# Loading and gating a linear recurrence by chunks of 1024 tokens instead of windows of 512

## The chip, the core and the metric

The kernel runs on one core of a Trainium2 chip. Its engines work side by side, each through a queue of its own, in order: TensorE (PE: matrix multiplies and transposes into PSUM; PEld is its loading of weights), VectorE (DVE), ScalarE (ACT), GpSimd (POOL) and SyncE (SP), which here only issues transfers. Sixteen DMA engines carry the transfers. They are tied together by semaphores. The metric is the device time of one execution in microseconds; the time of the kernel before is 302.48 us, the median of three runs (301.65 to 303.43).

## What is computed

The input has 4 sequences of 6336 tokens with 256 features, 25344 tokens in all. A gated linear recurrence runs along each sequence, and a gated unit with a causal convolution follows:

```python
sig_r, sig_i = 1/(1+exp(-r_gate)), 1/(1+exp(-i_gate))
a_t = exp(8 * sig_r * log(clip(a_base, 1e-6, 1-1e-6)))    # a_base = sigmoid(a_param), per feature
x_gated = sqrt(max(1 - a_t*a_t, 1e-6)) * sig_i * x
h = a_t[:, t] * h + x_gated[:, t];  y[:, t] = h            # for every token t, h starts at 0
gate = sigmoid(sum over k of conv_w[k] * y shifted)        # 5 taps, causal
out = (gate * (y @ w_val)) @ w_out
```

All inputs and the output are float32; the kernel works in bfloat16 between the stages.

## The kernel before

Tokens are cut into windows of at most 512 (`wins`, numbered 0 to 50) and windows into chunks (`CHUNKS`, L16): chunks 0 and 1 are one window of 256, chunk 2 one of 512, chunks 3 to 25 two windows of 512 each (windows 3 to 48), chunks 26 and 27 one window of 512 and one of 256. Work on the two gates' inputs and on the gated unit goes by windows, the recurrence by chunks. Sigmoids are computed as 0.5 + 0.5 tanh(x/2), so that tangent and exponential share one table of ScalarE; the square root needs another table, and `BATCHES` (L19) says which chunks share one visit to it.

The order of the work is written out by hand in `ORDER` (L33): one word for each step, with its window or chunk, the half of the features where there are two (.0 or .1), and behind an @ its PSUM banks. The loop at L504 emits the words one after the other, and every engine takes its own instructions in that order. It loads another table where the next word needs it (L509). The words:

- lr, li, lx (L276 to L283, `load` at L267): SP issues the load of a window of r, i or x, 512 KB each for 512 tokens, in pieces of 4 KB for each of 128 partitions (token 4p+j of the window lies in partition p). They go to two rings of four windows, `riring` and `xring`.
- th (L286): ACT takes the tangent of both gates of one window in one operation, 2048 columns of `riring` to `tring`. `tring` (L203) has three places of three halves for each window: `swapped` (L263) makes two successive windows of one place use them in turn, so that the tangents of r stay longer than those of i.
- pp (L295), up (L307): POOL adds 1 to the tangent of i and multiplies with x into `uring`, the ring of gated inputs, ten windows (`NU`). For some windows PE copies x to PSUM (xp, L311) and DVE does both in one operation (uv, L319).
- tr (L326), ex (L339): PE transposes the tangents of r to features by tokens, ACT takes the exponential into `aring`. `GROUPS` says which two chunks share one operation.
- sq on POOL, sa on ACT (L356, L364): the square of a. rt (L368): ACT takes the root for one batch.
- nt (L383), xg (L396), xt (L401): PE transposes the roots back to tokens by features, DVE multiplies them into `uring`, PE transposes the product.
- sc (L415): DVE runs the recurrence of a chunk as a scan, 1024 columns for each half.
- cv (L435), tg (L448), vl (L452), gv (L461), ou (L466): the convolution on PE, its tangent on ACT, y @ w_val on PE, the gate's product on DVE, the last product on PE, each for a window. cd or ca (L484, L487) copies the result out of PSUM, on DVE or on ACT, and st (L490) stores it, issued by SP.

A load waits until its place in the ring has been read: lr and li of a window for the tangent four windows back, lx for the product with x four windows back. A store waits for its copy, and loads behind it in SP's queue wait with it.

```python
    dst = riring[:, w % NRI, "ri".index(which) ^ swapped(w), 0:J, :]
nc.sync.dma_start(dst, flat[which][wstart[w]:wstart[w] + n, :].rearrange("(p j) d -> p j d", p=P))
...
nc.scalar.activation(out=tring[:, w % NTRI, a:a + 2, 0:J, :], in_=riring[:, w % NRI, :, 0:J, :],
                     func=ACT.Tanh, scale=0.5)
...
if table.get(name, have) != have:
    have = table[name]
    nc.scalar.preload_act_table_set(have)
```

Of the kernel before, what the change touches and what calls it, by code (L numbers as in the profile page):

```python
# [8 lines left out]
P = 128  # L9
# [14 lines left out]
NU = 10  # L24
NRI = 4
NX = 4
NTRI = 3
# [6 lines left out]
s_ident s_small s_kt s_diag li.2 lr.2 th.2 lr.3 lr.0 li.0 th.0 pp.0 tr.2.0@0 li.1 lr.1 tr.0.0@1 ex.2.0 th.1 lx.0 lx.2  # L34
li.3 up.0 tr.2.1@2 ex.2.1 tr.0.1@0 ex.0.0 tr.1.1@3 ex.1.1 tr.1.0@4 sq.1.1 ex.0.1 sq.0.1 lx.3 xp.3@0,1 lx.1 lr.6 th.3
sq.0.0 rt.0 lr.5 sq.2.0 pp.2 up.2 nt.0@5 xg.0 xt.0@2,3 li.5 th.5 sq.2.1 li.6 lr.4 uv.3 th.6 pp.6 pp.5 xp.1@5 sc.0.0
sc.0.1 cv.0@2,3 uv.1 li.4 th.4 tg.0 s_wl.1 ex.1.0 lx.4 li.7 tr.3.1@0,1 s_wl.0 lr.7 ex.3.1 lx.5 tr.3.0@2,3 ex.3.0
s_wl.3 lx.6 lx.7 pp.4 up.4 th.7 lr.9 rt.2 xp.7@2,3 li.8 uv.7 sa.4.0 sq.4.1 sq.3.1 sq.1.0 rt.1 nt.2@0 xg.2 nt.1@1 xg.1
s_wl.2 lr.8 li.10 lx.8 xt.2@2,3 xt.1@0,1 sc.1.1 li.9 lr.10 sq.3.0 rt.3 li.11 up.6 sc.1.0 lx.10 lr.11 sc.2.1 sc.2.0
up.5 th.8 lx.11 s_wcast th.10 lx.9 pp.10 up.10 lr.14 th.9 li.13 li.14 lr.13 xp.8@4,5 li.12 lr.12 uv.8 th.11 li.15  # L40
nt.3@0,1 xg.3 nt.4@6,7 pp.11 up.11 cv.1@2,3 tg.1 xg.4 xt.3@0,1 sc.3.1 vl.1@4,5 tr.5.0@6,7 ex.5.0 sq.5.0 tr.5.1@2,3
gv.1 ou.1.0@1 cd.1.0 st.1 lx.12 lr.15 ex.5.1 vl.0@4,5 xp.9@6,7 th.14 sq.5.1 cv.2@2,3 sc.3.0 th.13 uv.9 lx.13 xt.4@1,0
gv.0 ou.0.0@4 cd.0.0 st.0 sc.4.1 lx.15 cv.3@6,7 th.12 li.16 li.18 tr.7.1@4,5 tg.2 vl.2@2,3 gv.2 tg.3 ex.7.1 sq.6.1
sq.6.0 lx.14 pp.14 pp.12 up.12 tr.7.0@6,7 ex.7.0 sq.7.0 lx.16 cv.4@2,3 tg.4 th.15 ou.2.0@4,5 cd.2.0 sc.4.0 st.2 lr.18
lr.16 vl.3@6,7 xp.13@2,3 vl.4@4,5 gv.4 sq.7.1 rt.4 uv.13 th.16 sq.8.1 sq.8.0 pp.15 up.15 li.17 lr.17 up.14 ou.4.0@4,5
li.19 cv.5@0,1 lr.19 gv.3 cd.4.0 lx.17 tg.5 ou.3.0@6,7 lx.18 st.4 cd.3.0 st.3 nt.5@4,5 li.20 xg.5 pp.16 up.16 th.17
pp.17 lr.20 nt.7@6,7 xg.7 lx.19 li.21 nt.6@2,3 xg.6 th.18 pp.18 lr.21 xt.5@4,5 sc.5.1 up.17 vl.5@6,7 cv.6@0,1 tg.6
th.19 tr.9.1@2,3 ex.9.1 li.22 lr.22 up.18 sq.9.1 pp.19 gv.5 sc.5.0 tr.9.0@6,7 ex.9.0 lx.20 ou.5.0@0,1 cd.5.0 sq.10.1
xt.6@5,4 up.19 sc.6.1 cv.7@0,1 tg.7 cv.8@2,3 th.20 lr.24 tg.8 sc.6.0 vl.6@6,7 gv.6 xt.7@0,1 cv.9@4,5 ou.6.0@6,7 sc.7.0
th.21 tg.9 cd.6.0 vl.7@2,3 gv.7 vl.9@6,7 th.22 tr.11.0@0 sc.7.1 ou.7.0@2,3 vl.8@4,5 sq.9.0 tr.12.0@1 gv.9 ou.9.0@6,7  # L50
gv.8 ou.8.0@4,5 sq.10.0 st.5 cd.7.0 cd.9.0 lx.22 st.6 rt.5 lx.21 nt.8@6,7 lr.23 li.23 cd.8.0 nt.9@4,5 pp.22 pp.21
up.22 pp.20 up.20 up.21 xg.8 ex.12.0 xg.9 ex.11.0 li.24 st.7 st.9 li.25 lr.25 lx.23 lx.24 li.26 lr.26 th.23 xt.8@6,7
sc.8.0 sq.11.0 pp.23 sq.12.0 lr.27 li.27 cv.11@2,3 tg.11 cv.10@4,5 sc.8.1 cv.12@0,1 st.8 th.24 pp.24 tg.10 tg.12
vl.11@2,3 tr.11.1@6 ex.11.1 gv.11 vl.10@4,5 gv.10 th.25 xt.9@0,1 sc.9.0 tr.12.1@2 ex.12.1 ou.11.0@6,7 cd.11.0
ou.10.0@4,5 cd.10.0 cv.14@2,3 up.23 lx.25 lx.27 th.26 nt.10@6,7 sc.9.1 st.11 li.29 st.10 tg.14 tr.13.0@4,5 xg.10 up.24
sq.11.1 th.27 ex.13.0 tr.13.1@2,3 vl.12@0,1 gv.12 sq.12.1 li.30 lr.30 lx.26 pp.25 pp.27 sq.13.0 xt.10@6,7 sc.10.1
ex.13.1 sq.13.1 up.27 sq.14.0 pp.26 up.25 lr.28 cv.13@4,5 tg.13 vl.13@0,1 gv.13 li.28 vl.14@2,3 gv.14 ou.12.0@4,5
cd.12.0 ou.13.0@0,1 cd.13.0 ou.14.0@2,3 cv.15@4,5 lr.29 st.13 lx.28 lr.31 sc.10.0 cv.16@0,1 cd.14.0 rt.6 nt.11@6,7
tg.15 tg.16 xg.11 vl.15@2,3 gv.15 th.28 st.12 li.31 lx.29 sq.14.1 up.26 nt.13@4,5 xg.13 pp.28 up.28 nt.12@0,1 xg.12
li.32 vl.16@2,3 gv.16 lx.31 lr.32 lx.30 xt.11@4,5 sc.11.1 sc.11.0 ou.15.0@6,7 th.30 pp.30 th.29 pp.29 cv.18@0,1  # L60
ca.15.0 lr.34 li.34 up.29 cv.17@2,3 tg.18 xt.12@6,7 tg.17 vl.17@0,1 gv.17 tr.15.1@2,3 tr.15.0@4,5 th.31 sc.12.0
ou.17.0@0,1 cd.17.0 sc.12.1 ex.15.1 ex.15.0 cv.20@2,3 tg.20 li.33 lr.33 ou.16.0@0,1 cd.16.0 th.32 vl.18@4,5 gv.18
pp.31 up.31 th.34 xt.13@2,3 sc.13.1 vl.19@6,7 cv.19@0,1 tg.19 gv.19 st.17 st.14 st.16 st.15 up.30 th.33 sq.16.1 lx.32
sc.13.0 li.35 lr.35 lx.33 ou.18.0@4,5 cd.18.0 lx.34 li.36 sq.15.0 lr.38 cv.21@0,1 sq.15.1 vl.21@6,7 st.18 lx.35 lr.36
tg.21 gv.21 vl.20@0,1 sq.16.0 cv.22@2,3 gv.20 li.38 lr.37 li.37 pp.34 ou.19.0@4,5 cd.19.0 pp.33 pp.32 up.32
ou.21.0@6,7 ou.20.0@0,1 rt.7 cd.21.0 st.21 tg.22 cd.20.0 nt.14@4,5 xg.14 st.19 nt.16@6,7 xg.16 vl.22@0,1 gv.22 th.35
up.33 up.34 pp.35 tr.17.1@2,3 ex.17.1 xt.14@4,5 sc.14.0 sc.14.1 tr.17.0@6,7 ex.17.0 cv.23@0,1 cv.24@2,3 tg.23 tg.24
ou.22.0@6,7 cd.22.0 nt.15@0,1 xg.15 vl.24@2,3 vl.23@4,5 gv.23 st.20 st.22 lx.36 gv.24 up.35 cv.26@6,7 sq.17.1 th.36
pp.36 sq.18.0 th.38 xt.15@0,1 sc.15.0 sc.15.1 th.37 pp.37 sq.18.1 sq.17.0 ou.23.0@4,5 tg.26 ca.23.0 cv.25@2,3 tg.25
tr.19.0@6,7 ex.19.0 sq.19.0 xt.16@4,5 sc.16.0 tr.19.1@2,3 ex.19.1 sc.16.1 cv.27@0,1 ou.24.0@6,7 cd.24.0 tg.27  # L70
vl.25@2,3 vl.26@0,1 sq.19.1 rt.8 cv.28@4,5 gv.26 up.36 sq.20.1 li.39 st.23 lx.38 lr.40 pp.38 gv.25 lx.37 vl.27@6,7
gv.27 ou.26.0@0,1 cd.26.0 ou.25.0@2,3 lr.41 lr.39 tg.28 th.39 st.24 cd.25.0 ou.27.0@6,7 cd.27.0 nt.19@0,1 nt.17@2,3
xg.17 xg.19 cv.29@6,7 tg.29 sq.20.0 up.37 up.38 nt.18@4,5 xg.18 vl.28@2,3 gv.28 vl.29@6,7 gv.29 xt.17@0,1 sc.17.1
li.40 th.40 tr.21.1@4 li.41 th.41 pp.40 pp.39 st.26 st.25 tr.21.0@5 ex.21.1 ex.21.0 lx.39 li.42 ou.29.0@6,7 ca.29.0
lr.42 sc.17.0 st.27 lx.40 xt.18@2,3 up.39 th.42 ou.28.0@4,5 cv.30@6,7 cd.28.0 tg.30 tr.22.1@0 ex.22.1 tr.22.0@1
sq.21.0 sq.21.1 up.40 cv.32@6,7 ex.22.0 sq.22.1 tg.32 sc.18.1 cv.31@4,5 tg.31 lr.43 st.29 sc.18.0 li.43 th.43
vl.30@0,1 vl.31@6,7 gv.30 vl.32@4,5 gv.32 gv.31 ou.30.0@0,1 cd.30.0 xt.19@3,2 sc.19.0 ou.31.0@6,7 sq.22.0 rt.9
ou.32.0@4,5 st.28 cd.32.0 cd.31.0 lr.44 sc.19.1 lx.41 lx.43 lr.45 pp.42 pp.43 pp.41 up.41 li.44 up.43 lr.46 li.46
lx.42 up.42 st.30 cv.33@0,1 li.45 vl.33@4,5 tg.33 st.32 gv.33 nt.21@6,7 th.44 nt.20@0,1 xg.20 lx.45 lr.47 li.48 lr.48
th.46 pp.44 xg.21 nt.22@2,3 xg.22 lx.44 cv.35@4,5 th.45 pp.45 pp.46 up.45 st.31 li.47 ou.33.0@0,1 ca.33.0 tg.35  # L80
xt.20@6,7 sc.20.0 tr.23.1@2,3 ex.23.1 sc.20.1 cv.34@0,1 tg.34 cv.36@4,5 sq.24.1 tg.36 vl.35@2,3 gv.35 vl.36@0,1 gv.36
tr.23.0@6,7 vl.34@2,3 gv.34 ou.35.0@4,5 cd.35.0 lx.46 st.33 up.44 xt.21@0,1 sq.23.1 th.48 pp.48 ex.23.0 sq.24.0
sc.21.0 sc.21.1 th.47 cv.38@2,3 tg.38 ou.36.0@4,5 ou.34.0@6,7 ca.36.0 sq.23.0 ca.34.0 xt.22@2,3 tr.25.0@0 ex.25.0
sc.22.1 sq.25.0 tr.25.1@4 ex.25.1 sc.22.0 cv.37@6,7 tg.37 cv.39@0,1 tg.39 vl.40@4,5 vl.38@6,7 gv.38 sq.25.1 rt.10
st.35 li.49 st.36 vl.37@0,1 st.34 vl.39@2,3 lx.49 lr.49 lr.50 lx.48 gv.37 ou.38.0@6,7 cd.38.0 st.38 gv.39 cv.40@0,1
ou.37.0@6,7 cd.37.0 st.37 lx.47 nt.23@2,3 nt.24@6,7 tg.40 up.46 th.49 ou.39.0@0,1 ca.39.0 xg.23 xt.23@2,3 xg.24
cv.41@6,7 gv.40 ou.40.0@0,1 tg.41 ca.40.0 pp.49 pp.47 sc.23.1 cv.42@4,5 vl.41@0,1 sc.23.0 tg.42 gv.41 tr.26.0@3 li.50
ex.26.0 vl.42@6,7 st.39 up.47 th.50 xt.24@4,5 nt.25@2,3 gv.42 up.48 xg.25 st.40 ou.41.0@0,1 ca.41.0 st.41 cv.43@6,7
tg.43 vl.43@0,1 tr.27.0@2 tr.26.1@3 ex.26.1 ex.27.0 sc.24.0 gv.43 sc.24.1 ou.42.0@6,7 sa.27.0 ca.42.0 lx.50 st.42
xt.25@4,3 sc.25.0 tr.27.1@2 sq.26.1 ex.27.1 ou.43.0@0,1 ca.43.0 sq.27.1 st.43 cv.44@6,7 tg.44 sc.25.1 cv.45@0,1 tg.45  # L90
cv.46@6,7 tg.46 pp.50 vl.45@0,1 gv.45 vl.46@4,5 vl.44@6,7 up.50 sq.26.0 gv.46 gv.44 rt.11 cv.48@2,3 ou.45.0@0,1
# [8 lines left out]
def kernel(  # L100
# [30 lines left out]
    clen = [sum(CHUNKS[c]) for c in range(NCH)]  # L131
    cstart = [sum(clen[:c]) for c in range(NCH)]


    def places(cap, lens):
        at, out = 0, []
        for n in lens:
            if at + n > cap:
                at = 0
            out.append(at)  # L140
            at += n
        return out
# [398 lines left out]
```

## Time and profile before

| | |
|---|---|
| median of three runs | 302.48 us (301.65 to 303.43) |
| profiled execution | 300.32 us, of which the span of the trace is 298.5 us |
| busiest engines | ACT 278.8 us, DVE 247.6, PE 246.4, POOL 232.8 |
| moved by DMA | 104.75 MB, 351 GB/s over the span |
| tangents (L289) | 48 of 2048 columns, mean 1918 ns; 3 of 1024, mean 1050 ns |
| scans (L430) | 40 of 1024 columns, mean 2335 ns |
| table loads (L509) | 20, 1283 ns each |

The profile is of one execution. Busy time is the time in which an engine has at least one instruction running; back-to-back instructions of ACT and DVE overlap a little, so that the distance from start to start is shorter than the duration. The table's means are durations. "Idle before" an instruction is put down to the semaphore that came last. The chain of waits is followed back from the last instruction.

### The profile page before, as it was taken

The page shows a single profiled execution, that of the slowest core. Times are in us where ns is not written, and L with a number is a line of the kernel's source. Part 1 is how long each engine was busy: PE and PEld are TensorE (multiplying, and loading weights), DVE is VectorE, ACT ScalarE, POOL GpSimd, SP SyncE. Part 2 cuts the span into 40 slices and gives each one's busy share as a digit, 9 for nine tenths or more (in the row PEclk, how much of TensorE's full clock was granted, in tenths as well). Part 3 has the DMA queues.
Part 4 walks back from the last instruction along what each step waited for, and adds up shares of the span by engine and source line. Part 5 has one row for each costly group of instructions (what it writes and reads, how often), then busy time and mean ns, then how long its engine had stood idle before and what let it go on. Part 6 is the DMA issues. An engine that isn't in the chain of part 4 may idle for free.

```text
span 298.5 us, 6286 instructions
## 1 busy us (share of the span) xinstructions
PE 246.4 (83%) x2509; PEld 167.8 (56%) x2509; DVE 247.6 (83%) x206; ACT 278.8 (93%) x197; POOL 232.8 (78%) x155
## 2 busy tenths in 40 slices
PE   0374577897888598989898899998979999899993
PEld 0134255454556466757664758567647675666662
DVE  2030288849999889999999999999999899899993
ACT  6799999999999999999999999999999999969863
POOL 1478958989999899899999879998995996255300
PEclk9997599999999979999999999999999999999999
DMA  6999999999999999999999998999999977726046
GB/s 252 408 408 385 379 411 407 406 414 406 337 379 370 419 416 415 411 406 321 417 411 375 388 417 335 396 353 361 349 409 419 408 278 270 273 116 248 29 186 246
DMA packets 29995, 104.75 MB, mean 351 GB/s; under 512 B 3335, under 2 KB 3854, under 8 KB 29966
## 3 DMA queue, kind: packets, MB, share of 16 engines
q1 hardware_dynamic: 29952, 104.35, 90.5%
q8 instruction: 19, 0.31, 0.4%
q14 instruction: 10, 0.08, 0.1%
q10 hardware_dynamic: 14, 0.01, 0.0%
HBM read 78.39 MB, written 25.95 MB: 350 GB/s over the span
## 4 chain that ended last, share of the span: by engine, by line
ACT 31%; PE 23%; DVE 13%; issue 13%; DMA 12%; POOL 5%; SPq 1%; ACTq 0%; DVEq 0%; POOLq 0%
ACT tring L289 10%; ACT aring L350 8%; DMA riring<-in_r_gate_dram 7%; DVE yring L430 7%; PE banks L442 5%; ACT tgring L449 5%; PE banks L457 5%; ACT ering L377 4%; PE banks L472 4%; PE banks L392 3%; DMA riring<-in_i_gate_dram 3%; DVE tgring L462 3%; DVE oring L480 2%; DMA xring<-in_x_dram 2%; ACT L509 2%
## 5 line engine op out<-in xcount | busy, mean ns | idle before, releaser
L430 DVE TENSOR_TENSOR_SCAN yring<-aring,yring,banks 128x1024 bf16<-128x1024 f32 (+5 forms) x54 | 106.2, 1988 | 0.9 <-PE banks L408 0.6
L358 POOL TENSOR_TENSOR ering<-aring 128x1024 f32<-128x1024 f32 (+2 forms) x54 | 91.5, 1713 | 9.7 <-ACT aring L350 9.7
L309 POOL TENSOR_TENSOR uring<-tring,xring 128x1024 bf16<-128x1024 bf16 (+1 forms) x45 | 94.6, 2113 | 4.9 <-DMA xring<-in_x_dram 3.5
L289 ACT ACTIVATE tring<-riring 128x2048 bf16<-128x2048 f32 (+1 forms) x51 | 93.8, 1867 | 4.1 <-DMA riring<-in_i_gate_dram 1.9
L297 POOL TENSOR_SCALAR tring<-tring 128x1024 bf16<-128x1024 bf16 (+1 forms) x45 | 45.8, 1026 | 30.5 <-ACT tring L289 30.4
L442 PE MATMUL banks<-yring,diag 64*64 64x512 bf16 (+7 forms) x1080 | 61.9, 361 | 4.6 <-ACT aring L350 1.6
L462 DVE SCALAR_TENSOR_TENSOR tgring<-tgring,banks 128x1024 bf16<-128x1024 bf16 (+1 forms) x51 | 58.9, 1178 | 5.5 <-PE banks L457 4.4
L472 PE MATMUL banks<-wo,tgring 128*128 128x256 bf16 x396 | 51.4, 274 | 4.7 <-DVE tgring L462 3.5
L350 ACT ACTIVATE aring<-banks,khf 128x2048 f32<-128x2048 bf16 (+3 forms) x38 | 54.1, 1474 | 0.5 <-PE banks L334 0.4
L449 ACT ACTIVATE tgring<-banks 128x1024 bf16<-128x1024 f32 (+1 forms) x51 | 50.4, 1009 | 3.4 <-PE banks L442 3.3
L457 PE MATMUL banks<-yring,wv 128*128 128x512 bf16 (+4 forms) x216 | 49.4, 361 | 5.0 <-DVE oring L480 2.2
L472 PEld LDWEIGHTS <-tgring 128*128 128x128 bf16 x396 | 41.0, 114 | 15.7 <-DVE tgring L462 9.6
L442 PEld LDWEIGHTS <-diag 64*64 64x64 bf16 x1080 | 30.3, 106 | 28.8 <-issue 13.6
L377 ACT ACTIVATE ering<-ering 128x4096 bf16<-128x4096 f32 (+5 forms) x15 | 44.9, 3019 | 0.1
L399 DVE TENSOR_TENSOR uring<-banks,uring 128x2048 bf16<-128x2048 bf16 (+2 forms) x28 | 29.8, 1095 | 18.2 <-PE banks L392 17.9
L480 DVE COPY oring<-banks 128x1024 f32<-128x1024 f32 (+1 forms) x35 | 40.6, 1181 | 4.8 <-ACT aring L350 2.4
L334 PE MATMUL banks<-ident_b,tring 128*128 128x128 bf16 x396 | 29.0, 227 | 12.2 <-ACT tring L289 10.4
L334 PEld LDWEIGHTS <-tring 128*128 128x128 bf16 x396 | 25.1, 101 | 17.7 <-ACT tring L289 11.7
L457 PEld LDWEIGHTS <-wv 128*128 128x128 bf16 x216 | 19.7, 97 | 26.3 <-issue 12.4
L392 PE MATMUL banks<-ident,ering 128*128 128x128 f32 x198 | 28.8, 296 | 6.8 <-DVE oring L480 2.6
L392 PEld LDWEIGHTS banks<-ident,ering 128*128 128x128 f32 x198 | 25.9, 208 | 13.5 <-ACT ering L377 7.7
L408 PE MATMUL banks<-ident,uring 128*128 128x128 f32 x198 | 27.5, 282 | 2.6 <-DVE uring L399 2.5
(36 smaller groups left out, 113.1 us busy)
## 6 DMA issues: line engine op xcount, KB each, us to landing
riring<-in_i_gate_dram SPq DMA_DIRECT2D x48, 512.0 KB, 8.2
riring<-in_r_gate_dram SPq DMA_DIRECT2D x48, 512.0 KB, 8.3
xring<-in_x_dram SPq DMA_DIRECT2D x48, 512.0 KB, 8.0
out_dram<-oring SPq DMA_DIRECT2D x48, 512.0 KB, 5.7
riring<-in_r_gate_dram SPq DMA_DIRECT2D x3, 256.0 KB, 6.3
riring<-in_i_gate_dram SPq DMA_DIRECT2D x3, 256.0 KB, 6.5
xring<-in_x_dram SPq DMA_DIRECT2D x3, 256.0 KB, 5.3
out_dram<-oring SPq DMA_DIRECT2D x3, 256.0 KB, 7.3
```

What stands on the lines that cost most here:

```text
L289: nc.scalar.activation(out=tring[:, w % NTRI, a:a + 2, 0:J, :], in_=riring[:, w % NRI, :, 0:J, :], func=ACT.Tanh, scale=0.5)
L309: nc.gpsimd.tensor_tensor(out=u, in0=t1, in1=xt, op=ALU.mult)
L350: nc.scalar.activation(out=dst, in_=src, func=ACT.Exp, scale=khf[:, h:h + 1], bias=khf[:, h:h + 1])
L358: nc.gpsimd.tensor_tensor(out=e, in0=a, in1=a, op=ALU.mult)
L377: nc.scalar.activation(out=ering[:].bitcast(BF16)[:, 4 * o:4 * o + 2 * n], in_=ering[:, 2 * o:2 * o + 2 * n], func=ACT.Sqrt, scale=-0.25, ...
L392: nc.tensor.transpose(out=bank[:, k:k + P], in_=ering[:, e + q:e + wins[w] // 2:nq], identity=ident[:])
L430: nc.vector.tensor_tensor_scan(out=yring[:, h, col:col + o1 - o0], data0=aring[:, h, a_at[c] + o0:a_at[c] + o1], data1=xT[:, o0:o1], initi ...
L442: nc.tensor.matmul(out=gp[oh * 64:oh * 64 + 64, h, a:b], lhsT=diag[half * 64:half * 64 + 64, h, k, :], rhs=yring[half * 64:half * 64 + 64, ...
L449: nc.scalar.activation(out=tgring[:, w % NTG, :, 0:wins[w]], in_=live.pop(("gp", w))[:, :, 0:wins[w]], func=ACT.Tanh, scale=0.5)
L457: nc.tensor.matmul(out=val[:, m, a:b], lhsT=wv[:, hk, m * P:(m + 1) * P], rhs=yring[:, hk, col:col + b - a], start=(hk == 0), stop=(hk == ...
L462: nc.vector.scalar_tensor_tensor(out=tgring[:, w % NTG, :, 0:wins[w]], in0=tgring[:, w % NTG, :, 0:wins[w]], scalar=1.0, in1=live.pop(("va ...
L472: nc.tensor.matmul(out=ops[:, j * D:(j + 1) * D], lhsT=gv[:, hk, j:wins[w]:J], rhs=wo[:, hk, :], start=(hk == 0), stop=(hk == H - 1))
```

## The change

Loads and tangents of the two gates, and the loads of x, go by chunks. For a chunk of two windows lr, li and lx each move 1 MB in pieces of 8 KB a partition (token 8p+j of the chunk lies in partition p), and one th takes 4096 columns. There are 28 of each of these words instead of 51; they carry the number of the chunk's first window. `riring` and `xring` keep their size and are addressed as two halves, each for one long chunk or two short ones. `tring` has three halves, each with both gates of 1024 tokens (6 KB more a partition), and `swapped` is gone. `uring` has eight windows instead of ten (4 KB less a partition). pp, up, xp, uv and everything behind the scan still go by windows; the transposes (tr, nt, xt) take tokens in the new layout, with as many instructions for a chunk as before. `CHUNKS`, `BATCHES` and `GROUPS` are the same.

`ORDER` is new throughout. It has 18 ca and 33 cd (before 16 and 35), 6 sa and 50 sq (2 and 54), 5 uv with their xp (6), 46 pp and up (45), and the same 20 table switches. Its beginning, before and after, and the core of the code:

```diff
-NU = 10
+NU = 8
...
-NTRI = 3
+NTRI = 6
...
-s_ident s_small s_kt s_diag li.2 lr.2 th.2 lr.3 lr.0 li.0 th.0 pp.0 tr.2.0@0 li.1 lr.1 tr.0.0@1 ex.2.0 th.1 lx.0 lx.2
-li.3 up.0 tr.2.1@2 ex.2.1 tr.0.1@0 ex.0.0 tr.1.1@3 ex.1.1 tr.1.0@4 sq.1.1 ex.0.1 sq.0.1 lx.3 xp.3@0,1 lx.1 lr.6 th.3
...
+s_ident s_small s_kt s_diag li.0 li.1 lr.1 th.1 lr.0 th.0 tr.0.0@0 ex.0.0 tr.0.1@1 li.2 lr.2 lx.1 tr.1.1@2 tr.1.0@3
+lx.0 lr.3 pp.0 up.0 pp.1 lx.2 li.3 ex.1.0 ex.1.1 ex.0.1 sa.0.1 sa.0.0 sa.1.1 th.2 lr.5 li.5 tr.2.0@1 sq.1.0 up.1 lx.3
+rt.0 nt.0@0 xg.0 rt.1 nt.1@2 xt.0@3,0 sc.0.0 sc.0.1 ex.2.0 th.3 pp.4 xg.1 tr.2.1@4 ex.2.1 li.7 lr.7 sq.2.0 xt.1@3,2
...
+    def slots(cap, lens):
+        at, out = 0, []
+        for n in lens:
+            at += at % n
+            if at + n > cap:
+                at = 0
+            out.append(at)
+            at += n
+        return out
...
+    ri_at = places(NRI, [len(z) for z in CHUNKS])
+    x_at = places(NX, [len(z) for z in CHUNKS])
+    t_at = slots(NTRI, [len(z) for z in CHUNKS])
...
-        riring = rings.tile([P, NRI, 2, 4, D], FP32, name="riring")
-        xring = rings.tile([P, NX, 4, D], FP32, name="xring")
-        tring = rings.tile([P, NTRI, 3, 4, D], BF16, name="tring")
+        riring = rings.tile([P, NRI // 2, 16, D], FP32, name="riring")
+        xring = rings.tile([P, NX // 2, 8, D], FP32, name="xring")
+        tring = rings.tile([P, NTRI // 2, 16, D], BF16, name="tring")
...
         def load(w, which):
-            n = wins[w]
-            J = n // P
+            c = chunk_of[w]
+            J = clen[c] // P
             if which == "x":
-                dst = xring[:, w % NX, 0:J, :]
+                dst = x_in(c)[:, 0:J, :]
             else:
-                dst = riring[:, w % NRI, "ri".index(which) ^ swapped(w), 0:J, :]
-            nc.sync.dma_start(dst, flat[which][wstart[w]:wstart[w] + n, :].rearrange("(p j) d -> p j d", p=P))
+                dst = gates_in(c)[:, "ri".index(which), 0:J, :]
+            nc.sync.dma_start(dst, flat[which][wstart[w]:wstart[w] + clen[c], :].rearrange("(p j) d -> p j d", p=P))
...
         def op_th(w):
-            J = wins[w] // P
-            a = swapped(w)
-            nc.scalar.activation(out=tring[:, w % NTRI, a:a + 2, 0:J, :], in_=riring[:, w % NRI, :, 0:J, :],
-                                 func=ACT.Tanh, scale=0.5)
+            c = chunk_of[w]
+            J = clen[c] // P
+            nc.scalar.activation(out=slot(tring, t_at, c)[:, :, 0:J], in_=gates_in(c)[:, :, 0:J], func=ACT.Tanh, scale=0.5)
```

Around windows 7 to 15, where the prediction counts rooms, the new order has, with the words of ACT, SP and POOL that matter here: th.5 li.9 lr.9 ... tg.1 uv.2 lx.5 tg.0 ... ex.3.1 ... ex.3.0 ... th.7 th.9 rt.2 ... lx.7 lr.11 li.11 sq.4.0 lr.13 li.13 rt.3 ... uv.6 lx.9 nt.2 ... th.11 li.15 lr.15 ... sc.3.0 ... th.13 ... th.15.

## The prediction

> **What bounds the kernel now.** I read the busy line of the page, then the busy time by stage, ScalarE's waits, its queue in order of time, and last the transfers.
>
> ```profile
> PE 246.4 (83%) x2509; PEld 167.8 (56%) x2509; DVE 247.6 (83%) x206; ACT 278.8 (93%) x197; POOL 232.8 (78%) x155
> ```
>
> ```profile
> 100.00:140.00 40.00, 34.98 (x367) 25.80 (x366) 36.68 (x31) 39.38 (x26) 38.44 (x23) 0.96 1.02 396
> 140.00:180.00 40.00, 36.96 (x401) 25.16 (x400) 39.80 (x33) 39.94 (x26) 36.32 (x23) 1.00 1.02 402
> 180.00:220.00 40.00, 37.11 (x410) 26.46 (x412) 39.20 (x28) 39.91 (x27) 37.66 (x24) 1.00 0.97 363
> 220.00:260.00 40.00, 36.07 (x408) 25.24 (x396) 37.95 (x31) 39.78 (x28) 28.25 (x17) 1.00 0.89 341
> 260.00:298.00 38.00, 33.91 (x360) 22.02 (x352) 32.62 (x27) 25.98 (x28) 11.88 (x10) 1.00 0.43 168
> ```
>
> The columns are the stretch, its length, busy time of PE, PEld, DVE, ACT and POOL, PE's granted clock, DMA share and GB/s. Until 260 us ACT has no free time, DVE and POOL hardly any, and PE 3 to 5 us in each 40. After 260 us ACT and DVE have holes and PE is the busiest. So ACT's queue sets the pace of the middle, and PE that of the end; in the chain of waits the last 25 us are mostly PE:
>
> ```profile
> 273.84 2.36 PE banks L442 x40
> 276.24 2.75 PE banks L457 x12
> 278.99 1.21 PE banks L442 x20
> 280.19 1.00 PE banks L472 x8
> ```
>
> ACT's waits are small, and those for loads add to 3.3 us, all before 47 us:
>
> ```profile
> ACT oring L482 <- PE banks L472: 6.3, 5, 1.8
> ACT tgring L449 <- PE banks L442: 3.3, 7, 1.0
> ACT tring L289 <- DMA riring<-in_i_gate_dram: 1.9, 2, 1.7
> ACT tring L289 <- DMA riring<-in_r_gate_dram: 1.4, 2, 0.8
> ```
>
> **The tangents (th).** What an operation costs a full queue is the distance to the next start, not its own duration, since neighbours overlap by about 0.1 us:
>
> ```profile
> 10.85 1.04 ACT L289 ACTIVATE tring<-riring 128x1024 bf16<-128x1024 f32 x1
> 11.79 2.13 ACT L350 ACTIVATE aring<-banks,khf 128x512 f32<-128x512 bf16 x4
> ...
> 78.29 3.70 ACT L289 ACTIVATE tring<-riring 128x2048 bf16<-128x2048 f32 x2
> 81.89 1.01 ACT L449 ACTIVATE tgring<-banks 128x1024 bf16<-128x1024 f32 x1
> ```
>
> A tangent of 1024 columns takes 0.95 us of the queue, one of 2048 takes 1.80 (3.60 for two). The step of 0.85 per 1024 gives 3.50 for 4096. Two of 2048 cost 3.60, so each merged pair saves 0.10. There are 23 pairs: **-2.3 us** of ACT. The busy column would have promised more (2 x 1.918 against 3.65, 0.18 each), but the overlap is already had. A 4096-wide tangent is not in the trace: the bounds are 3.60 (no saving) and 3.42 (0.18 saved), so 0 to -4.2 us; I take the line through the starts.
>
> **What the new order moves between engines.** The copies out of PSUM go from 35 on DVE and 16 on ACT to 33 and 18; a copy of 1024 columns on ACT holds the queue 0.91 us, and one short copy (0.49) goes to DVE: 18 x 0.91 - (15 x 0.91 + 0.49) = **+2.2 us** of ACT. Squares on ACT go from 2 (0.95 and 0.33) to 6 (five of 0.33, one of 0.54): **+0.9**. The 20 table switches between exponential and root, the roots, exponentials and gate tangents are the same. ACT's work comes out at -2.3 + 2.2 + 0.9 = **+0.8 us**: what the merge saves is spent again. DVE loses three long copies, gets a short one, and loses one L323 operation (-3.4 + 0.6 - 0.6 = -3.4 us); PE loses one 0.62 us multiply of L314; POOL changes by 0.3. DVE's gain lies beside a full ACT, and I count nothing for it.
>
> **The rings.** Eight slots of gated inputs hold four chunks instead of five, and the tangents' ring holds three chunks instead of one and a half (for i; about three for r). Before, POOL waited 30 us for tangents and ACT only 0.5 for POOL to free one, so I cost both at nothing; without that cover a wait of ACT on a ring would cost its full length.
>
> **The start.** Here the transfers bound both kernels:
>
> ```profile
> 7.46:14.90 7.44, 2.26 (x16) 1.46 (x16) 0.00 (x0) 5.71 (x9) 3.13 (x5) 1.00 1.04 409
> 14.90:22.40 7.50, 5.82 (x16) 2.37 (x20) 2.96 (x7) 6.91 (x6) 5.54 (x5) 1.00 1.03 409
> 37.30:52.20 14.90, 10.61 (x100) 8.18 (x101) 12.49 (x14) 14.30 (x9) 10.40 (x10) 1.00 1.03 408
> ```
>
> The share of the DMA engines is 1.0. I summed the bytes in the order of SyncE's queue and set them on these rates, plus 1.4 us for the last piece (th.0 started at 9.22 with 2.1 MB ahead, 8.0 by the rates). In the new order th.5 needs 7.3 MB (22.3 us), th.9 12.6 MB (36.0), th.13 19.4 MB (52.8). ACT's own work ahead of them sums to 15.3, 27.2 and 44.3 us, so the queue runs 7.0, 8.8 and 8.5 us behind its bare work, 8.8 at most. Before it is 8.5 (th.8 has 32.4 us of work ahead of it and starts at 40.87). **+0.3 us.**
>
> **The pipeline behind it.** The first root over long chunks (rt.3) ends at about 45.4 us, since two chunks' tangents now come ahead of it (39.6 before). Then the first long scan starts at about 50.5 (46.5 before). PE priced by its rows (L442 x20 1.21, L457 x4 0.87, L472 x8 0.90, L392 and L408 2.0 and 1.74 per 1024 tokens, L334 0.90 per 16, L314 0.62 each) has 246.0 us listed behind sc.3.0 before, and that took from 51.5 to 298.5, 247 us; after, 251.4 are listed behind the same point, 1 us earlier: PE is 4.4 us late. POOL has 206.2 us listed behind it (195.6 before), part of which it can work off earlier, and waits some 2 us for lx.9 (20.4 MB, about 55 us); it has room at the end, where it is busy 11.9 us of 38. DVE is level, ACT 1.1 late, which is the +0.8 and +0.3 above. The 15 us that PE stands free between 100 and 260 us can take in part of its 4.4. Bounds: all is taken in (0) or nothing (+4.4 - 1.1 = +3.3 beyond ACT's part); I take **+2.0**, as two more chunks must pass PE while ACT leaves it no pause.
>
> **Sum.** -2.3 + 2.2 + 0.9 + 0.3 + 2.0 = +3.1 us on the span of 298.5; the profiled execution took 300.3 (1.8 around the span), so 303.4 for it. The median of the runs shown, 302.48, lies 2.2 above that execution: **305.5 us**, 1% slower. Differences below 0.5% are about what a measurement of this kernel can't tell from none.
>
> **Rivals.**
>
> Loads come too late (slower). The tangent of a chunk now waits for 2 MB, and their slot comes free only after the tangent two chunks back. ACT's work between the two is 8.4 us for th.9 (two gate tangents of 0.5, two exponentials of 1.95, one tangent of 3.5), 10.1 for th.37, 10.2 for th.45, 10.3 for th.15, 11.0 for th.21. The price of a load:
>
> ```profile
> riring<-in_i_gate_dram SPq DMA_DIRECT2D x48, 512.0 KB, 8.2
> ...
> riring<-in_i_gate_dram SPq DMA_DIRECT2D x3, 256.0 KB, 6.5
> ```
>
> 1.7 us for 256 KB more makes 11.6 for 1 MB; it decides where the room is below 11.6. These five chunks are short by 0.6 to 3.2 us, 8.0 in all (the earlier ones are in the start above; root batches give the others 12 us and more, up to 37). Against it: queues are shorter where transfers are less dense, and before, rooms of 8.0 and 9.2 us cost nothing. 8.0 + 0.8 + 0.3 = 9.1 us, time **311.6**.
>
> The end gets shorter (faster). At rt.10, which starts at about 248 us in both if ACT alone decides (243.9 us of work ahead of it and its switches, against 244.3), PE has 45.7 us listed behind it, 49.6 before; those took 50.3. If PE is really that far, the end comes 3.9 us earlier: **298.5**. Against it: between rt.9 and rt.10 the order lists 36.5 us of PE and only 26.7 of ACT (32.2 and 32.1 before), which PE can't do in that time.
>
> Larger pieces move faster. The page's best slices, with pieces of 4 KB, reach 421 GB/s:
>
> ```profile
> GB/s 252 408 408 385 379 411 407 406 414 406 337 379 370 419 416 415 411 406 321 417 411 375 388 417 335 396 353 361 349 409 419 408 278 270 273 116 248 29 186 246
> ```
>
> If all of the start ran at 421 instead of 408, the 19.4 MB ahead of th.13 would land 1.5 us sooner and the forecast would be **304.0**, at the bound of no change. The Trainium skill, DMA: Bandwidth & Descriptors, section Bandwidth, asks for transfers of at least 1 MiB and tables 341 GB/s for 1 MB and 425 for 16 MB; an estimate from its 425 would be 1.9 us instead of 1.5. The trace speaks against a gain: 512 KB transfers already make 408, because many are in flight at once.
>
> It cancels (no change): the merge saves 0.1 each, other work fills it, PE's free time takes in the later start: **302.5**. And should a tangent of 4096 cost as much as two (the change doesn't do what it says), 2.3 are added to the forecast: 307.8, inside its own range.
>
> **Chances.** Forecast 0.35 (304 to 309), late loads 0.18, shorter end 0.30, larger pieces 0.04, cancelled 0.13. So faster 0.30, same 0.17, slower 0.53. With both signs held, the range reaches from below the shorter end to beyond the late loads: 297 to 314.
>
> **What would show it.** A tangent of 4096 should start its successor 3.50 us later. ACT should wait for loads about 5 us, all before 55 us; waits of th on riring later than that are the first rival. rt.3 should end near 45 us, sc.3.0 start near 50.5. If rt.9 starts near 221 us (215.8 before) and rt.10 clearly after 250, PE sets the pace and the forecast is right; rt.10 near 248 and an end 46 us later is the second. I am wrong if ACT has idle time in the middle for another reason, such as a ring of gated inputs that is too short.

## The result, and the profile after

The changed kernel takes 305.51 us, median of four runs (304.89 to 307.63), against 302.06 in the four runs of the kernel before beside it. The ratio is **1.0144**, interval 1.0105 to 1.0183: slower by 1.4%, clear of the interval. The profiled execution took 304.89 us with a span of 303.1, 4.6 us more than before. Ratios are taken over runs in the chip's faster state; one of the four runs of e2_split and three of the six of e7_loads_first, the profiled one among them, were counted in the slower one, so for these two the ratio says more than the median.

The page's busy line, and the busy time by stage of the changed kernel (columns as in the prediction):

```profile
PE 243.1 (80%) x2482; PEld 166.6 (55%) x2507; DVE 244.1 (81%) x203; ACT 280.2 (92%) x180; POOL 232.5 (77%) x153
```

```profile
100.00:140.00 40.00, 33.18 (x374) 23.85 (x379) 38.92 (x32) 39.91 (x23) 39.83 (x24) 1.00 1.00 389
140.00:180.00 40.00, 34.79 (x364) 23.48 (x364) 37.42 (x30) 37.07 (x21) 34.79 (x22) 1.00 0.99 369
180.00:220.00 40.00, 34.34 (x391) 24.40 (x388) 36.04 (x25) 38.84 (x24) 36.06 (x22) 1.00 0.99 393
220.00:260.00 40.00, 36.25 (x411) 25.19 (x414) 38.28 (x30) 38.92 (x24) 35.12 (x22) 1.00 0.76 282
260.00:303.00 43.00, 37.67 (x376) 25.27 (x380) 35.13 (x30) 31.39 (x34) 11.95 (x9) 0.98 0.53 201
```

ACT is busy 1.4 us longer in all, though it has 17 instructions fewer, and from 140 us on it is no longer full: 37.07 and 38.84 us of 40, where it had 39.94 and 39.91. DVE loses busy time in the same stretches (37.42 and 36.04 against 39.80 and 39.20). PE's figures are put too low by this profile, in which 25 matmul records are missing (2482 to 2507 weight loads). So 4.6 us are 1.4 of work and 3.2 of idle time on ACT. What it waited for, by the waits of ACT, its four longest groups:

```profile
ACT tring L310 <- DMA riring<-in_r_gate_dram: 4.6, 4, 1.5
ACT oring L502 <- PE banks L492: 4.1, 5, 1.2
ACT tgring L469 <- DVE uring L418: 2.4, 1, 2.4
ACT tring L310 <- DMA riring<-in_i_gate_dram: 1.8, 2, 1.1
```

Loads account for 6.4 us, 3.3 before, 3.1 more; the other waits differ too, but their differences nearly cancel (the 2.4 us for VectorE are new and lie in the end, those for the products and convolutions of TensorE are shorter). The places of the waits for loads, and what a tangent of 4096 columns costs, are in ACT's queue in order of time (the number in brackets is the idle time before the instruction):

```profile
76.44 3.62 ACT L310 ACTIVATE tring<-riring 128x4096 bf16<-128x4096 f32 x1
79.96 1.92 ACT L469 ACTIVATE tgring<-banks 128x1024 bf16<-128x1024 f32 x2
...
148.66 3.62 ACT L310 ACTIVATE tring<-riring 128x4096 bf16<-128x4096 f32 x1 [1.53 <-DMA riring<-in_r_gate_dram]
...
179.10 3.62 ACT L310 ACTIVATE tring<-riring 128x4096 bf16<-128x4096 f32 x1 [1.22 <-DMA riring<-in_r_gate_dram]
...
212.46 3.62 ACT L310 ACTIVATE tring<-riring 128x4096 bf16<-128x4096 f32 x1 [1.08 <-DMA riring<-in_i_gate_dram]
```

The long tangent holds the queue 3.52 us. The tangents of chunks 17, 20 and 23 (th.31, th.37, th.43) wait for a load, 3.8 us together, in the middle, where the kernel before waits for none. The loads themselves:

```profile
riring<-in_r_gate_dram SPq DMA_DIRECT2D x23, 1024.0 KB, 9.2
riring<-in_i_gate_dram SPq DMA_DIRECT2D x23, 1024.0 KB, 10.3
xring<-in_x_dram SPq DMA_DIRECT2D x23, 1024.0 KB, 10.5
```

A load of 1 MB lands 9.2 to 10.5 us after its issue (medians), one of 512 KB did after 8.0 to 8.3.

### The profile page after: what moved, and what is told of

The parts are those of the page before. It is cut to its first block, busy times and chain, and to the rows that moved or that the text cites. A ratio compares the mean times of both kernels' runs of the same rounds, so it can differ in the third digit from the quotient of the medians.

```text
span 303.1 us, 6125 instructions
## 1 busy us (share of the span) xinstructions
PE 243.1 (80%) x2482; PEld 166.6 (55%) x2507; DVE 244.1 (81%) x203; ACT 280.2 (92%) x180; POOL 232.5 (77%) x153
## 4 chain that ended last, share of the span: by engine, by line
ACT 23%; DMA 22%; PE 17%; POOL 14%; issue 11%; DVE 10%; SPq 1%; ACTq 0%; DVEq 0%; POOLq 0%
DMA xring<-in_x_dram 12%; ACT tring L310 8%; POOL ering L380 7%; DMA riring<-in_i_gate_dram 6%; PE banks L462 5%; DVE yring L450 4%; ACT ering L399 4%; POOL uring L334 4%; PE banks L492 4%; ACT aring L372 4%; DVE tgring L482 4%; PE banks L477 4%; ACT tgring L469 3%; POOL tring L317 3%; DVE uring L418 2%
## 5 line engine op out<-in xcount | busy, mean ns | idle before, releaser
L334 POOL TENSOR_TENSOR uring<-tring,xring 128x1024 bf16<-128x1024 bf16 (+1 forms) x46 | 95.5, 2092 | 14.2 <-DMA xring<-in_x_dram 13.7
L380 POOL TENSOR_TENSOR ering<-aring 128x1024 f32<-128x1024 f32 (+2 forms) x50 | 89.8, 1820 | 11.6 <-ACT aring L372 11.6
L310 ACT ACTIVATE tring<-riring 128x4096 bf16<-128x4096 f32 (+2 forms) x28 | 90.1, 3225 | 6.6 <-DMA riring<-in_r_gate_dram 4.6
L462 PE MATMUL banks<-yring,diag 64*64 64x512 bf16 (+7 forms) x1080 | 63.0, 366 | 4.6 <-ACT tgring L469 1.8
L477 PE MATMUL banks<-yring,wv 128*128 128x512 bf16 (+7 forms) x191 | 48.2, 358 | 6.9 <-ACT tgring L469 2.0
L462 PEld LDWEIGHTS <-diag 64*64 64x64 bf16 x1080 | 29.0, 108 | 31.0 <-issue 14.5
L500 DVE COPY oring<-banks 128x1024 f32<-128x1024 f32 (+1 forms) x33 | 37.6, 1164 | 5.1 <-PE banks L492 3.0
L411 PE MATMUL banks<-ident,ering 128*128 128x128 f32 x198 | 30.1, 297 | 5.9 <-ACT ering L399 2.3
## 6 DMA issues: line engine op xcount, KB each, us to landing
xring<-in_x_dram SPq DMA_DIRECT2D x23, 1024.0 KB, 10.5
```

Of the source, the lines that this page charges most:

```text
L310: nc.scalar.activation(out=slot(tring, t_at, c)[:, :, 0:J], in_=gates_in(c)[:, :, 0:J], func=ACT.Tanh, scale=0.5)
L334: nc.gpsimd.tensor_tensor(out=u, in0=t1, in1=xt, op=ALU.mult)
L380: nc.gpsimd.tensor_tensor(out=e, in0=a, in1=a, op=ALU.mult)
L411: nc.tensor.transpose(out=bank[:, k:k + P], in_=ering[:, e + q:e + half:half // P], identity=ident[:])
L462: nc.tensor.matmul(out=gp[oh * 64:oh * 64 + 64, h, a:b], lhsT=diag[half * 64:half * 64 + 64, h, k, :], rhs=yring[half * 64:half * 64 + 64, ...
L477: nc.tensor.matmul(out=val[:, m, a:b], lhsT=wv[:, hk, m * P:(m + 1) * P], rhs=yring[:, hk, col:col + b - a], start=(hk == 0), stop=(hk == ...
```

## The experiments

Each is compared with runs of the kernel before on the same chip; the changed kernel itself stands at 1.0144 of it. Theories A and B are on what sets the pace: A, ScalarE's queue; B, TensorE and VectorE, with ScalarE's waits beside them. C, D and E are on the late loads: C, loads that come earlier only make others later; D, the bytes ahead of them make them late; E, the stores ahead of them in SyncE's queue do.

**e1_hoist.** Four loads earlier in SyncE's queue.

```diff
-li.31 lx.27 ... st.15 ... st.14 ... lr.31
+li.31 lr.31 lx.27 ... st.15 ... st.14
-li.37 ... st.20 ... lr.37
+li.37 lr.37 ... st.20
-li.41 lr.41 th.41 ... st.27 lx.37 st.25 lr.43 li.43
+li.41 lr.41 th.41 ... lr.43 li.43 st.27 lx.37 st.25
```

> Only the order of four loads changes: lr.31 and lr.37 are issued next to li.31 and li.37, ahead of a load of x and one or two stores, and both loads of chunk 23 ahead of two stores and a load of x. Theory A (ScalarE's queue sets the pace, and its three waits for loads after 55 us, 1.53 + 1.22 + 1.08 us, are paid in full): the waits go, ScalarE comes to the last root batch 3.8 us earlier, time 305.5 - 3.8 = 301.7 (301.5 to 303). Theory B (TensorE and VectorE set the pace behind sc.3.0, ScalarE's waits lie beside their work): 305 to 306. Theory C (the loads only change places: x comes later): GpSimd waits for x more than 13.7 us, time 305 to 308.

Measured: 306.37 us, ratio 1.0153 (1.0094 to 1.0212): nothing gained. ScalarE's waits in its profile:

```profile
ACT tring L309 <- DMA riring<-in_r_gate_dram: 3.2, 4, 1.5
ACT tring L309 <- POOL uring L333: 2.9, 2, 2.4
```

and GpSimd's:

```profile
POOL uring L333 <- DMA xring<-in_x_dram: 15.8, 6, 5.8
```

The waits of th.31 and th.43 for loads are gone, that of th.37 is 0.86 instead of 1.22 and th.39 has a new one of 0.51. In exchange x comes later, GpSimd waits up to 5.8 us for it (15.8 in all, 13.7 in the changed kernel), and ScalarE then waits 2.9 us for GpSimd to free a place of `tring`. The wait was moved, as theory C had it.

**e2_split.** The long tangent in two operations of 2048 columns, one for each gate.

```diff
-            nc.scalar.activation(out=slot(tring, t_at, c)[:, :, 0:J], in_=gates_in(c)[:, :, 0:J], func=ACT.Tanh, scale=0.5)
+            for k in range(2 if J == 8 else 1):
+                half = slice(k, k + 1) if J == 8 else slice(0, 2)
+                nc.scalar.activation(out=slot(tring, t_at, c)[:, half, 0:J], in_=gates_in(c)[:, half, 0:J], func=ACT.Tanh, scale=0.5)
```

> Each long tangent is made in two operations of 2048 columns, one for each gate; loads and order stay. Theory A: 23 operations more at 0.08 to 0.10 us of ScalarE's queue each (a tangent of 4096 holds the queue 3.52 us, two of 2048 hold it 3.60), so +2 us, time 307.5. Theory B: within 0.5 us of 305.5. If the durations counted in full (2 x 1.918 against 3.624), +4.9 us, 310.4.

Measured: 308.31 us, ratio 1.0244 (1.0184 to 1.0303), 1.0% above the changed kernel, 3 us. The two intervals all but touch, and one of the four runs, the profiled one, took 304.61 us, as little as the changed kernel. So the sign is that of theory A and ScalarE's busy time rose by 1.6 us (281.8), but the size is open.

**e3_halves.** Every 1 MB load as two of 512 KB, pieces of 4 KB.

```diff
-            nc.sync.dma_start(dst, flat[which][wstart[w]:wstart[w] + clen[c], :].rearrange("(p j) d -> p j d", p=P))
+            src = flat[which][wstart[w]:wstart[w] + clen[c], :].rearrange("(p j) d -> p j d", p=P)
+            for j in range(0, J, 4):
+                nc.sync.dma_start(dst[:, j:min(j + 4, J)], src[:, j:min(j + 4, J)])
```

> Each load of 1 MB is issued as two of 512 KB in pieces of 4 KB; the chunk's tangent still waits for all of them, but the first window's x can be used when its half has landed. Theory A: pieces of 8 KB gain nothing, since 512 KB loads already ran at 408 GB/s in the start; the gates arrive as before, time 305.5 within 1, GpSimd's wait for x falls from 13.7 to below 9 us without moving the time. Rival (the larger pieces carry faster, or the 69 more issues of 0.42 us hold SyncE up): 307 or more.

Measured: 307.14 us, ratio 1.0165 (1.0105 to 1.0225), not to be told from the changed kernel. Pieces of 8 KB are worth nothing that can be measured here. GpSimd's wait for x stayed at 13.3 us: the expectation that half a chunk of x would help it was wrong. ScalarE's waits for the gates stayed too (6.6 us), as a tangent still needs the whole chunk.

**e4_copies.** Six copies out of PSUM from VectorE to ScalarE.

```diff
-cd.12.0 cd.14.0 cd.18.0 cd.20.0 cd.22.0 cd.24.0
+ca.12.0 ca.14.0 ca.18.0 ca.20.0 ca.22.0 ca.24.0
```

> Six copies out of PSUM (windows 12, 14, 18, 20, 22, 24) move from VectorE to ScalarE: 6 x 0.91 = 5.5 us more for ScalarE, 6 x 1.14 = 6.8 less for VectorE. Theory A (ScalarE's queue sets the pace): 305.5 + 5.5 = 311. Theory B (VectorE or TensorE set it): 305.5 or less.

Measured: 310.82 us, ratio 1.0316 (1.0262 to 1.0371), 1.7% or 5.2 us above the changed kernel, for 5.5 us of work. What ScalarE is given in the middle is paid in full (its busy time rises by 5.2 us), though VectorE's falls by 5.5.

**e5_stores_after, e6_stores_before.** One token in four is stored, in both kernels.

```diff
-of[wstart[w]:wstart[w] + n, :].rearrange("(p j) d -> p j d", p=P), oring[:, w % NOSB, 0:J, :]
+of[wstart[w]:wstart[w] + n, :].rearrange("(p j) d -> p j d", p=P)[:, 0:1], oring[:, w % NOSB, 0:1, :]
```

> The changed kernel stores one token in four (a quarter of a long window's output), so three quarters of the output are left out: 19.5 MB fewer of 104.7 MB, with the same waits of SyncE for the copies. The run before showed that loads issued earlier only move the wait to x. Theory D (the transfers are what comes late: the DMA engines are full from 10 to 220 us, and ScalarE's 6.4 us and GpSimd's 13.7 us of waits for loads come from the bytes ahead of them): both waits fall by more than half, time 305.5 - 4 = 301.5 or less. Theory E (SyncE's queue is what comes late: loads stand behind stores that wait for their copies, 152 us in all): the waits stay, time 304.5 to 305.5.

> The same cut of the stores in the kernel before (three quarters of the output left out). ScalarE waits there for loads only in the first 47 us, before the first store, so theories A and D both expect within 1 us of its own time (301.5 to 302.5); if fewer stores help it by as much as the changed kernel, the transfers are not what tells the two apart.

Measured: 300.58 us, ratio 0.9972 (0.9939 to 1.0005), and 298.95 us, ratio 0.9930 (0.9906 to 0.9954). The changed kernel gains 1.7%, the kernel before 0.7% (more than the 1 us that was expected). Between them 0.4% is left of 1.4%, with intervals that overlap. ScalarE's waits for loads in the changed kernel with fewer stores:

```profile
ACT tring L310 <- DMA riring<-in_r_gate_dram: 3.6, 3, 1.8
...
ACT tring L310 <- DMA riring<-in_i_gate_dram: 1.4, 2, 0.7
```

These 5.0 us all lie ahead of 55 us; the three of the middle are gone. Theory D had expected both waits to fall by more than half: GpSimd's for x did (13.7 to 5.7 us), ScalarE's only in the middle (6.4 to 5.0 in all). A load of 1 MB lands after 7.4 to 8.0 us instead of 9.2 to 10.5, and the span is 299.1, 4.0 us less than 303.1. SyncE waits for copies as before (148.8 us, 152.0 in the changed kernel), so theory E by itself doesn't explain the late loads. About 1 of the 1.4% thus hangs on the bytes that the stores move beside the loads (theory D): with a fifth fewer bytes the coarse loads of the middle are in time. Whether it is the gates or x that costs the time, the run doesn't separate.

**e7_loads_first.** Loads ahead of stores wherever the rings let them, from chunk 6 on.

```diff
-li.15 lr.15 st.1 lx.11 lx.13 st.2 st.0 lr.17 li.17 lr.19 li.19 st.4 st.3 lx.15 li.21 lr.21 st.5 lr.23 li.23 lx.17 st.6
+li.15 lr.15 st.1 lx.11 lx.13 lr.17 li.17 lr.19 li.19 st.2 st.0 lx.15 li.21 lr.21 st.4 st.3 lr.23 li.23 lx.17 st.5 lx.19 st.6
...
```

> From chunk 6 on each load stands as early in the order as its ring lets it, ahead of stores whose copies come later; the order of the loads among themselves and of the stores among themselves, and all other engines' orders, stay. Theory E (stores in SyncE's queue hold the loads): ScalarE's three waits after 55 us (3.8 us) and most of GpSimd's 13.7 us go, time 301.5 to 303. Theory D (bytes): the waits stay within 2 us of what they were, time 305 to 306.5.

Measured: 330.83 us, ratio 1.0920 (1.0856 to 1.0984), far outside both expectations. SyncE's waits tell why:

```profile
SPq L294 <- ACT tring L309: 85.5, 22, 11.9
SPq L512 <- DVE oring L499: 56.5, 17, 12.4
SPq L512 <- ACT oring L501: 48.1, 14, 8.4
SPq L294 <- POOL uring L333: 37.7, 9, 9.8
```

and VectorE's longest:

```profile
DVE oring L499 <- DMA out_dram<-oring: 24.1, 5, 10.4
```

SyncE (SPq) stands 123 us before loads whose place isn't free (tangents 85.5, products 37.7; 41.3 and 7.8 in the changed kernel), with finished stores queued behind. The output ring fills, VectorE's copies wait 24.1 us for a store to leave it (2.1 in the changed kernel), and ScalarE's exponentials wait 9.9 us for transposes, 7.5 of it right behind VectorE's longest wait. The gates do come in time (one wait of 0.25 us is left behind 55 us), but the place of the stores among the loads is no mistake that can be mended by putting loads first. That some loads stand behind stores is not refuted by this run.

**e8_windows.** Loads by 512 KB and tangents by window, in the changed kernel's layout, rings and order: the loads of e3_halves, and

```diff
-            nc.scalar.activation(out=slot(tring, t_at, c)[:, :, 0:J], in_=gates_in(c)[:, :, 0:J], func=ACT.Tanh, scale=0.5)
+            for j in range(0, J, 4):
+                part = slice(j, min(j + 4, J))
+                nc.scalar.activation(out=slot(tring, t_at, c)[:, :, part], in_=gates_in(c)[:, :, part], func=ACT.Tanh, scale=0.5)
```

> Loads by 512 KB and tangents by 2048 columns (both gates of one window, as in the kernel before), in the changed kernel's layout and order: the first window's tangent needs only half of the chunk's bytes, and its half of the ring is free 1.8 us earlier. ScalarE gets 23 x 0.08 to 0.10 = 2 us more work. If the late gates come from the size of the pieces that are waited for (the first rival of the prediction), the waits after 55 us go: -3.8 + 2 = 303.7. If they come from the order and the bytes: 305.5 + 2 = 307.5.

Measured: 305.45 us, ratio 1.0156 (1.0120 to 1.0192), the changed kernel's own time and neither of the two that were expected. The lines that matter, of the page and of ScalarE's waits:

```profile
PE 242.9 (80%) x2482; PEld 165.7 (55%) x2507; DVE 244.2 (81%) x203; ACT 281.7 (93%) x203; POOL 232.5 (77%) x153
```

```profile
ACT tgring L473 <- PE banks L466: 2.8, 5, 1.9
...
ACT tring L314 <- DMA riring<-in_r_gate_dram: 1.8, 2, 1.1
ACT tring L314 <- DMA riring<-in_i_gate_dram: 1.1, 2, 0.7
```

Waits for loads fall from 6.4 to 2.9 us, all ahead of 37 us. So the size of the tangent is what makes the gates late: it waits for a whole chunk, and it frees its place of the ring only at its end (the run doesn't tell the two apart). But the time isn't won: of the 3.5 us ScalarE's busy time takes back 1.5, and its waits for the convolution rise from 0.8 to 2.8, 1.94 of it in one wait that ends at 164.25 us. What is left against the kernel before, with tangents and loads as small as there, is the order, the rings and the layout of the tokens: 1.6%, of which 2.9 us of ScalarE's busy time (281.7 against 278.8).

**e9_copies_back, e10_windows_copies, e11_before_copies.** Copies given from ScalarE to VectorE: four in the changed kernel, the same four in e8_windows, three in the kernel before.

```diff
-ca.11.0 ca.16.0 ca.23.0 ca.29.0        # e9, e10
+cd.11.0 cd.16.0 cd.23.0 cd.29.0
-ca.15.0 ca.23.0 ca.29.0                # e11, the kernel before
+cd.15.0 cd.23.0 cd.29.0
```

> The changed kernel with its four copies on ScalarE before the last third (windows 11, 16, 23, 29) given back to VectorE: ScalarE 4 x 0.91 = 3.6 us less, VectorE 4 x 1.14 = 4.6 more. Theory A (ScalarE's queue sets the pace, as the run with six copies more had it: +5 us for 5.5): 305.5 - 3.6 = 302 (301.5 to 303). Rival (VectorE, 36 to 39 us busy of 40 between 100 and 220 us, has no room): 305 or more.

> Loads by 512 KB and tangents by 2048 columns in the changed kernel's layout and order (the run before it: no wait of ScalarE for loads after 37 us, ratio 1.0156), and the same four copies on VectorE. ScalarE's work is then that of the kernel before within 0.5 us and its waits are as few. Theory A: the time of the kernel before within 1 us (ratio 0.997 to 1.005); what is left over it is what the new order and the ring of eight cost by themselves. Rival (VectorE): ratio 1.015 or more.

> The kernel before, with its copies of windows 15, 23 and 29 on VectorE instead of ScalarE: 2.7 us less for ScalarE, 3.4 more for VectorE. Theory A without regard to VectorE: 301.3 - 2.7 = 298.6. Rival (VectorE is busy 39 of 40 us between 140 and 220 us in this kernel and has no room): 302 to 305.

Measured: 308.88 us, ratio 1.0225 (1.0192 to 1.0257); 308.49, 1.0201 (1.0169 to 1.0233); 310.01, 1.0258 (1.0225 to 1.0291). None is faster than what it was made from: the first and the last are slower by about 0.8 and 2.6%, the second by 0.4, within its interval. Theory A alone falls: ScalarE's busy time did fall by 2.0 us in the last one (276.8 against 278.8), and then it stood still. Its longest group of waits and one of TensorE's:

```profile
ACT aring L349 <- PE banks L333: 9.1, 6, 5.0
```

```profile
PE banks L407 <- DVE oring L479: 6.3, 2, 3.6
```

Its longest waits, 4.96 us before 151.7 and 2.65 before 192.5, stand before exponentials that need transposes. Shortly ahead of each, TensorE had waited for a copy of VectorE, 3.56 us before 147.4 and 2.73 before 190.5, and these transposes stand behind that wait in its queue. Three copies of 1.2 us cost 8. At these places VectorE had no more room than ScalarE.

**e12_no_xp6.** Window 6's product on GpSimd, so that TensorE doesn't stand 11 us before lx.5.

```diff
-li.13 rt.3 up.5 xp.6@4,5 uv.6 lx.9
+li.13 rt.3 up.5 pp.6 up.6 lx.9
```

> The changed kernel with window 6's product made on GpSimd (pp, up) instead of TensorE and VectorE (xp, uv): TensorE loses its 11.1 us wait for lx.5 at 28 us and 2 of its 0.62 us multiplies, VectorE 1.3 us, GpSimd gets 3.2 us more. The prediction's step of +2.0 us (TensorE, late behind sc.3.0, sets the pace): 1.5 to 2 us less, 303.7. Theory A: TensorE's lateness lies beside ScalarE, 305.5 within 0.7; GpSimd's 3.2 us more would rather make it slower.

Measured: 306.18 us, ratio 1.0143 (1.0113 to 1.0173): no change. The first line of TensorE's waits tells why:

```profile
PE banks L410 <- ACT ering L398: 17.1, 3, 14.8
```

TensorE now stands up to 14.8 us before the transposes of a root that ScalarE hasn't computed yet. Its wait for x lay beside that one, and the first long scan starts at 52.5 us (51.4 in the changed kernel), so x doesn't set when the pipeline starts. The run leaves TensorE's list behind sc.3.0 as it was, so by itself it doesn't settle what that list costs.

## Why the prediction was right, and where it wasn't

The forecast was 305.5 us and slower by 1%; measured are 305.51 and 1.4%. That the two times meet is luck. The span was forecast at 298.5 + 3.1 = 301.6 us and is 303.1, 1.5 too little; then 2.2 were added between the profiled execution and the median, which in the changed kernel lie 0.6 apart, 1.6 too much. And of the 3.1, the 2.0 of the pipeline stand on a step that the runs don't bear out.

- **The tangents: right.** 3.50 us of the queue was expected for 4096 columns, 3.52 is measured, so the merge saves 0.08 to 0.10 each and not the 0.18 of the durations. e2_split has the sign; its 3 us, where 2 were expected, are too uncertain to give a size.
- **Copies and squares on ScalarE, +3.1: right in size.** Busy time of ScalarE rose by 1.4 us where the work was counted as +0.8 (by 1.1 and 0.7 in e1_hoist and e5_stores_after, whose ScalarE does the same work). e4_copies shows that such copies are paid (5.2 us for 5.5). What the prediction left out is the other side: by e9 and e11 VectorE couldn't have taken such copies either. (That GpSimd had hardly any free time until 260 us is too strong, it is busy 28.25 us of 40 from 220 us on; nothing in the sum hangs on it.)
- **The start: right in time, not in its waits.** The root batch rt.3 ended at 45.9 us (45.4 expected) and sc.3.0 began at 51.4 (50.5 expected). The waits for loads in the first 55 us are th.0/th.1 0.63, th.5 0.70, th.9 1.25, together 2.6 us, where about 5 were expected, and none later.
- **The pipeline behind it, +2.0: wrong.** The step held that TensorE, late by 4.4 us at sc.3.0, sets the pace. Its own sign came true: rt.9 starts at 224.49 us (near 221 was expected) and rt.10 at 253.07, clearly after 250; and the 251.4 us listed for TensorE behind sc.3.0 meet the 251.7 that the changed kernel takes from there to its end. But the list isn't the time that TensorE needs. In the kernel before it waits 22 us for other engines behind sc.3.0, in the very stretch that its list of 246.0 us was said to fill, and in the changed kernel 26. In e5_stores_after, TensorE's list is that of the changed kernel, and from sc.3.0 (52.0 us) to the end (299.1) it takes 247.1 us, as in the kernel before. And from rt.9 to rt.10, where the list gives TensorE 36.5 us and ScalarE 26.7, the changed kernel takes 28.6. e12_no_xp6 only exchanged one wait of TensorE for another and doesn't settle it. In the place of the step the trace has ScalarE's three waits for loads, 3.8 us, which are the sign that the prediction gave for its first rival.
- **That rival, the late loads: right mechanism, wrong chunks and price.** It came to 311.6 us, with 8.0 of waits. 11.6 us to land was estimated, 9.2 to 10.5 is measured; of the chunks that the rooms named, th.9 (1.25 us) and th.37 (1.22) waited, th.15, th.21 and th.45 did not, and th.31 and th.43 waited though their rooms, counted in the same way, were 19.9 and 19.3 us: their loads stood in SyncE's queue behind a load of x and stores (lr.31 was issued at 137.9 us, its place had been free since 126.9). The room on ScalarE was the wrong thing to count alone; the place in SyncE's queue belongs to it.
- **The shorter end: wrong, as the forecast said.** rt.10's first table load is at 253.07 us against 248.21, and from there the end takes 50.0 us, 50.3 before, not the 46 that the shorter list behind it promised. This is the same fault, a list of TensorE taken for its time.
- **Larger pieces: no gain**, by e3_halves, as the rates of the start had said.

By ScalarE's queue, then, the 4.6 us of span are 1.4 of work, 3.8 of waits for loads in the middle and 0.6 less of all other waits. That about this much hangs on late loads is what e5 and e6 show: without those waits the span is 4.0 us shorter, of which the kernel before gains 1.8 with fewer stores too, and by the ratios 0.4 of the 1.4% are left. e8 shows that the gates are late because a tangent takes a whole chunk. But e1 and e8 show too that taking these waits away by themselves wins nothing: in e1 a wait for x comes in their place, in e8 the work of the smaller tangents and a wait for the convolution. So how the price splits between late gates and late x is open. Not settled either is how much of e8's 1.6% is the ring of eight, the order or the layout; no run takes them apart. GpSimd never waits for a place in `uring` in the changed kernel's trace, which speaks against the ring as the cause, though the order was written for eight places.

## What to carry to other kernels

Where an engine's queue is full, an operation costs the distance to the next start, so merging two saves only what doesn't overlap, here 0.1 us; a merged operation also waits for all of its input, and that can cost more. Count for a load both the time since its place came free and what stands ahead of it in the queue that issues it. In this schedule two engines were nearly full, and giving work from one to the other cost time in both directions; there only a smaller total can help. And a list of an engine's work, priced by its rows, isn't the time that it needs: look how long the engine waits in the same stretch.

## What the runs showed of the hardware that was not expected

- A load of 1 MB took only 0.9 to 2.5 us longer to land than one of 512 KB in the kernel before (9.2 to 10.5 against 8.0 to 8.3 us), less than the 3.4 that the step from 256 to 512 KB suggested; against the 512 KB loads of e3_halves, in the same order (8.6 to 9.4 us), it was 0.3 to 1.7.
- The landing time follows what else is moved: with three quarters of the output not stored, the same 1 MB loads landed after 7.4 to 8.0 us.
- Three copies of 1.2 us, put into VectorE's queue where it was nearly full (39.80 and 39.20 us busy of 40), cost 8 us.
